# A fallback path written as a loop over short stretches, in place of unrolled blocks

## Chip, cores, metric

One core of a Trainium2 chip. The metric is the device time of one execution in microseconds (us), the median over several runs of the slowest core (here the only one). The "span" of a profile is the stretch from the first to the last recorded instruction; it is 1.5 to 2.1 us shorter than the device time of the same run.

## The reference, cut to what matters

```python
# x, f_logit: (4, 6080, 256); w_in: (256, 2048); w_out: (2048, 256)
f = lower_bound + (1 - lower_bound) * sigmoid(f_logit)
for t in range(S):                     # one recurrence along each sequence
    h = f[:, t] * h + (1 - f[:, t]) * x[:, t]
    y[:, t] = h
z = y.reshape(24320, 256) @ w_in       # 24320 tokens
out = (z - tanh(z)) @ w_out
```

Below, "h" means what the kernel calls h, the product z. For small z the kernel replaces z - tanh(z) by a short polynomial in z squared, which is exact enough; for large z it needs tanh. As built the polynomial is the cheaper way: the whole output takes 2333 us by it.

## The kernel before

It has two parts. `fast()` computes the whole output by the polynomial, and while doing so ScalarE sums max(h*h - TINY, 0) into `flags`. At the end the sum is one number, `flag`. If it is not zero, some h was too large, and `general()` computes the whole output again with tanh.

```python
TINY = 0.03
...
        def watch(n, i):
            t = half(n, i, "t")                      # h squared
            junk = sumpool.tile([P, 2, 2, HB], BF16, name="junk")
            nc.scalar.activation(
                out=junk[:, :, :, 0 : st[n]["hb"]], in_=t, func=AF.Relu, bias=-TINY,
                accum_out=flags[:, 2 * n + i : 2 * n + i + 1],
            )
...
        def end(j):                                  # the last block's output
            ...
                (nc.scalar.copy, nc.vector.tensor_copy)[half](
                    out=rows.rearrange("p i (m k) -> p i k m", k=KC), in_=bank[:]
                )
                t0 = starts[j] + half * hb
                nc.sync.dma_start(
                    out=out[t0 : t0 + hb, :].rearrange("(i p) d -> p i d", p=P), in_=rows
                )
...
    fast()
    seen = nc.values_load(flag[:].bitcast(INT32), ...)   # every engine loads the flag
    with tc.If(seen != 0):                               # every engine branches
        general()
```

`general()` runs over 48 blocks of up to 512 tokens, all unrolled in the program: 10705 instructions as built, of 23005 in all.

Of the kernel before, what the change touches and what calls it, by code (L numbers as in the profile page):

```python
# [9 lines left out]
FP32 = mybir.dt.float32  # L10
ALU = mybir.AluOpType
# [6 lines left out]
P = 128  # L18
# [13 lines left out]
def kernel(  # L32
# [25 lines left out]
    nc = tc.nc  # L58

    B, S, D = x.shape  # L60
    DFF = moe_w_in.shape[1]
    N = B * S
    KC = D // P
    TB = 512
    HB = TB // 2
    NQ = TB // P
    NU = DFF // TB
    H = 32
    G = P // H
# [4 lines left out]
    sizes = [HB] + [TB] * (N // TB)  # L74
    PLAIN, TURNED = 2, 2
    starts = [sum(sizes[:j]) for j in range(len(sizes))]
    NBLK = len(starts)
    srcs = [a.rearrange("b s d -> (b s) d") for a in (f_logit, x)]

    const = ctx.enter_context(tc.tile_pool(name="const", bufs=1))  # L80
    lb = const.tile([P, KC], FP32, name="lb")
# [832 lines left out]
    @with_exitstack  # L914
    def general(ctx):


        fetch, steps, ys = recurrence(ctx)[0:3]
        wpool = ctx.enter_context(tc.tile_pool(name="w", bufs=1))
        tpool = ctx.enter_context(tc.tile_pool(name="tpool", bufs=2))  # L920
        gpool = ctx.enter_context(tc.tile_pool(name="gpool", bufs=3))
        opool = ctx.enter_context(tc.tile_pool(name="opool", bufs=2))
        ps_h = ctx.enter_context(tc.tile_pool(name="ps_h", bufs=3, space=PSUM))
        ps_o = ctx.enter_context(tc.tile_pool(name="ps_o", bufs=1, space=PSUM))
        w_in = [wpool.tile([P, 2, 2, 2 * P], FP32, name=f"w_in{u}") for u in range(NU)]
        w_out = [wpool.tile([P, 2, 2, D], FP32, name=f"w_out{u}") for u in range(NU)]

        def temp(tag, dtype=FP32):
            return tpool.tile([P, 2, 2, HB], dtype, name=tag, tag=tag)

        with tc.manual_schedule():
            for u in range(NU):
                for fetch_w, w in ((fetch_w_in, w_in[u]), (fetch_w_out, w_out[u])):
                    raw = tpool.tile([P, KC * TB], INT64, name="raw", tag="raw")
                    fetch_w(u, raw[:], nc.gpsimd)
                    rounding = to_float32(
                        [(w[:].rearrange("p a b c -> p (a b c)"), lambda a: a)], raw[:],
                        lambda n: temp(dict(e="t", m="q", r="th")[n])[:].rearrange(
                            "p a b c -> p (a b c)"
                        ),  # L940
                    )
                    for step in ("ce", "cr", "cx", "cm", "cs", "cb", "cw"):
                        rounding[step]()
            for j, nb in enumerate(sizes):
                ns = nb // P
                fetch(j, queue=nc.gpsimd)
                for step in ("tf", "tx", "sg", "f0", "f1", "v0", "v1", "sc0", "sc1"):
                    steps[step](j)
                ps = ps_o.tile([P, NQ, D], FP32, name="psO")
                for u in range(NU):  # L950
                    for s in range(2):
                        hT = ps_h.tile([P, 2, TB], FP32, name="hT")
                        for c in range(2):
                            for k in range(KC):
                                nc.tensor.matmul(
                                    hT[:, c, 0:nb],
                                    lhsT=w_in[u][:, k, s, c * P : (c + 1) * P],
                                    rhs=ys[j][:, k, 0:nb],
                                    start=(k == 0),
                                    stop=(k == KC - 1),  # L960
                                )
                        h = hT[:, :, 0:nb]
                        t, th, q, small = [
                            temp(n)[:].rearrange("p a b c -> p a (b c)")[:, :, 0:nb]
                            for n in ("t", "th", "q", "small")
                        ]
                        gT = gpool.tile([P, 2, TB], FP32, name="gT")
                        g = gT[:, :, 0:nb]
                        nc.scalar.activation(out=t, in_=h, func=AF.Square)
                        nc.scalar.activation(out=th, in_=h, func=AF.Tanh)  # L970
                        nc.scalar.activation(
                            out=q, in_=t, func=AF.Square, scale=QA, bias=QB
                        )
                        nc.scalar.activation(
                            out=small, in_=t, func=AF.Relu, scale=-1.0, bias=SMALL
                        )
                        nc.vector.tensor_tensor(out=g, in0=h, in1=th, op=ALU.subtract)
                        nc.vector.scalar_tensor_tensor(
                            out=q, in0=q, scalar=QC, in1=th, op0=ALU.add, op1=ALU.mult
                        )  # L980
                        nc.vector.tensor_tensor(out=q, in0=q, in1=t, op=ALU.mult)
                        nc.vector.copy_predicated(
                            out=g, mask=small.bitcast(INT32), data=q
                        )
                        for c in range(2):
                            for i in range(ns):
                                nc.tensor.matmul(
                                    ps[:, i, :],
                                    lhsT=gT[:, c, i * P : (i + 1) * P],
                                    rhs=w_out[u][:, s, c, :],  # L990
                                    start=(u == s == c == 0 and i % 2 == 0),
                                    stop=(u == NU - 1 and s == c == 1),
                                    skip_group_check=True,
                                )
                osb = opool.tile([P, NQ, D], FP32, name="osb")
                nc.scalar.copy(out=osb[:, 0:ns, :], in_=ps[:, 0:ns, :])
                nc.gpsimd.dma_start(
                    out=out[starts[j] : starts[j] + nb, :].rearrange(
                        "(i p) d -> p i d", p=P
                    ),  # L1000
                    in_=osb[:, 0:ns, :],
                )

    fast()
    seen = nc.values_load(
# [3 lines left out]
    with tc.If(seen != 0):  # L1009
        general()  # L1010
# [32 lines left out]
```

## Time and profile before

| | before |
|---|---|
| device time, 3 runs | 2331.93, 2332.53, 2333.46 us |
| TensorE | busy 2319.6 us of a span of 2329.3; granted clock 1.00 |
| VectorE, ScalarE | busy 91% and 77% |
| instructions of `general()` executed | 0 |
| last output transfer | issued at 2324.4, landed 3.75 us later |

Some figures below have two decimals where a printed line has one. They are the start times of the same records in the trace, read to the nanosecond. One execution differs from the next by more than a microsecond (the spans of the changed kernel were 2329.9 to 2331.7 us), so for the last microseconds I do not compare spans. I compare distances inside one trace: from the issue of the last transfer to its landing, and to the end.

### The profile page before, as it was taken

To read this page: it belongs to the slowest core of one execution; us is meant where nothing else is said; L and a number is where in the kernel's file an instruction comes from. 1 tells how busy PE (TensorE), PEld (TensorE's weight loads), DVE (VectorE), ACT (ScalarE), POOL (GpSimd) and SP (SyncE) were. 2 spreads that over 40 slices of the span, in tenths; PEclk is the share of its full clock that TensorE was granted. 3 is DMA by queue.
4 is the path that set the end of the run, shared out by engine and by line. 5 is a ranking of instruction groups with operands and counts; after the bars stand their busy time and mean duration, and the time that the engine had idled before them with its cause. 6 is when DMAs were issued, how large, how long until landed. Compare 5 with 4: busy or idle time off the path is not lost.

```text
span 2329.3 us, 28648 instructions
## 1 busy us (share of the span) xinstructions
PE 2319.6 (100%) x10677; PEld 2025.2 (87%) x10677; DVE 2121.4 (91%) x2447; ACT 1801.1 (77%) x2686; POOL 0.7 (0%) x6
## 2 busy tenths in 40 slices
PE   9999999999999999999999999999999999999998
PEld 6888888888888888888888888888888888888887
DVE  8999899998999989999999999999899998999987
ACT  7677777777777777787777777777777777777775
POOL 0000000000000000000000000000000000000000
PEclk9999999999999999999999999999999999999999
DMA  6311211111111111112111121111211112111101
GB/s 172 64 24 32 42 37 28 28 35 39 37 28 28 37 36 37 28 28 42 32 37 28 28 45 28 37 28 28 46 29 36 28 28 46 31 33 28 28 10 29
DMA packets 296932, 85.05 MB, mean 37 GB/s; under 512 B 289872, under 2 KB 292688, under 8 KB 296784
## 3 DMA queue, kind: packets, MB, share of 16 engines
q1 hardware_dynamic: 296640, 83.14, 16.9%
q8 instruction: 85, 1.39, 0.2%
q14 instruction: 63, 0.52, 0.1%
q10 hardware_dynamic: 144, 0.00, 0.0%
HBM read 58.20 MB, written 24.90 MB: 36 GB/s over the span
## 4 chain that ended last, share of the span: by engine, by line
PE 99%; DMA 0%; SPq 0%; DVE 0%; issue 0%
PE A L383 27%; PE Qd L466 14%; PE Qa L466 14%; PE Qb L466 14%; PE D L383 14%; PE Qc L466 7%; PE B L383 7%; PE Qc L749 1%; PE Qb L749 1%; PE Qa L749 1%; PE A L682 1%; PE D L682 0%; PE Qd L682 0%; DMA xn<-in_x_dram 0%; PE B L682 0%; PE Qc L682 0%
## 5 line engine op out<-in xcount | busy, mean ns | idle before, releaser
L383 PE MATMUL A<-T,w_in 128*128 128x256 f32 x2208 | 558.8, 379 | 0.0
L383 PEld LDWEIGHTS A<-T,w_in 128*128 128x128 f32 x2208 | 419.5, 190 | 57.0
L427 DVE TENSOR_TENSOR h<-h,q 128x1024 f32<-128x1024 f32 x368 | 437.7, 1220 | 3.1
L421 DVE SCALAR_TENSOR_TENSOR q<-q,t 128x1024 f32<-128x1024 f32 x368 | 440.2, 1217 | 0.0
L414 ACT ACTIVATE q<-t 128x1024 f32<-128x1024 f32 x368 | 382.8, 1053 | 46.3 <-DVE h L427 43.4
L411 ACT ACTIVATE t<-h 128x1024 f32<-128x1024 f32 x368 | 388.7, 1057 | 3.1 <-DVE h L398 0.3
L432 ACT ACTIVATE junk<-t 128x1024 bf16<-128x1024 f32 x368 | 388.2, 1055 | 1.5
L446 DVE TENSOR_TENSOR Tg<-h 128x1024 f32<-128x1024 f32 x368 | 348.1, 946 | 6.4
L466 PE MATMUL Qb<-h,w_out 128*128 128x256 f32 x1472 | 347.7, 379 | 0.0
L466 PEld LDWEIGHTS Qb<-h,w_out 128*128 128x128 f32 x1472 | 279.7, 190 | 38.0
L466 PE MATMUL Qa<-Tg,w_out 128*128 128x256 f32 x736 | 219.0, 379 | 0.0
L466 PE MATMUL Qd<-h,w_out 128*128 128x256 f32 x736 | 219.0, 379 | 0.0
L466 PE MATMUL Qa<-h,w_out 128*128 128x256 f32 x736 | 218.9, 379 | 0.0
L466 PE MATMUL Qd<-Tg,w_out 128*128 128x256 f32 x736 | 218.9, 379 | 0.0
L395 ACT COPY h<-B 128x512 f32<-128x512 f32 x184 | 107.0, 582 | 143.2 <-PE B L383 94.4
L395 ACT COPY h<-A 128x512 f32<-128x512 f32 x184 | 107.3, 583 | 136.7 <-PE A L383 125.3
L398 DVE TENSOR_TENSOR h<-D,r 128x512 f32<-128x512 f32 x184 | 126.9, 690 | 92.9 <-PE D L383 90.8
L398 DVE TENSOR_TENSOR h<-A,r 128x512 f32<-128x512 f32 x184 | 126.3, 687 | 74.3 <-PE A L383 42.5
L395 ACT COPY r<-A 128x512 f32<-128x512 f32 x184 | 107.3, 583 | 105.9 <-PE A L383 105.9
L383 PE MATMUL D<-y,w_in 128*128 128x256 f32 x736 | 188.9, 379 | 0.0
L383 PE MATMUL B<-y,w_in 128*128 128x256 f32 x736 | 188.9, 379 | 0.0
L383 PE MATMUL A<-y,w_in 128*128 128x256 f32 x736 | 188.9, 379 | 0.0
(120 smaller groups left out, 3069.8 us busy)
## 6 DMA issues: line engine op xcount, KB each, us to landing
xn<-in_x_dram SPq DMA_DIRECT2D x184, 128.0 KB, 3.2
fn<-in_f_logit_dram SPq DMA_DIRECT2D x184, 128.0 KB, 3.1
out_dram<-osb SPq DMA_DIRECT2D x180, 128.0 KB, 2.8
raw<-in_moe_w_in_dram SPq DMA_DIRECT2D x8, 512.0 KB, 4.6
raw<-in_moe_w_out_dram SPq DMA_DIRECT2D x8, 512.0 KB, 4.8
out_dram<-osb SPq DMA_DIRECT2D x3, 256.0 KB, 3.7
fn<-in_f_logit_dram SPq DMA_DIRECT2D x1, 512.0 KB, 6.9
xn<-in_x_dram SPq DMA_DIRECT2D x1, 512.0 KB, 7.7
```

The lines of the kernel that those rows point to most:

```text
L383: nc.tensor.matmul(ps[:, c], lhsT=w_in[u][:, slot, c * P : (c + 1) * P], rhs=mixes[j][right], start=start and c == 0, stop=True, skip_grou ...
L395: nc.scalar.copy(out=dst, in_=piece(n, bank))
L398: nc.vector.tensor_tensor(out=piece(n, "h")[:, q], in0=piece(n, bank), in1=piece(n, r), op=ALU.add)
L411: nc.scalar.activation(out=half(n, i, "t"), in_=half(n, i), func=AF.Square)
L414: nc.scalar.activation(out=half(n, i, "q"), in_=half(n, i, "t"), func=AF.Square, scale=RA, bias=RB,)
L421: nc.vector.scalar_tensor_tensor(out=q, in0=q, scalar=RC, in1=t, op0=ALU.add, op1=ALU.mult)
L427: nc.vector.tensor_tensor(out=h, in0=h, in1=q, op=ALU.mult)
L432: nc.scalar.activation(out=junk[:, :, :, 0 : st[n]["hb"]], in_=t, func=AF.Relu, bias=-TINY, accum_out=flags[:, 2 * n + i : 2 * n + i + 1],)
L446: nc.vector.tensor_tensor(out=o, in0=a, in1=b, op=ALU.subtract)
L466: nc.tensor.matmul(acc[j, part][:, r, 0 : st[n]["hb"]], lhsT=w_out[u][:, slot, c * P : (c + 1) * P], rhs=piece(n, right)[:, q, c], start=( ...
L682: nc.tensor.matmul(h[c], lhsT=w_in[u][:, 2 * k + s, c * P : (c + 1) * P], rhs=ys[j][:, k, 0:nb], start=k == 0 and (c == 0 or len(banks) == 2),
L749: nc.tensor.matmul(acc[j][i // 2][:, i % 2].rearrange("p (k m) -> p k m", k=2), lhsT=plain[j, u][:, s, c, i * P : (i + 1) * P], rhs=w_out[ ...
```

## The change

The intent: the fallback path need not be 48 unrolled blocks. It becomes a hardware loop of 190 iterations, each taking 32 time steps of all four sequences (128 tokens), with the recurrence's state carried in a tile. `fast()` and the test are not touched. The core of the diff:

```diff
+    ALL = len(sizes)
+    sizes.append(B * H)                 # after NBLK = len(starts)
...
-            for j, nb in enumerate(sizes):
-                ns = nb // P
-                fetch(j, queue=nc.gpsimd)
-                for step in ("tf", "tx", "sg", "f0", "f1", "v0", "v1", "sc0", "sc1"):
-                    steps[step](j)
+            nc.vector.memset(carry[:], 0.0)
+        with tc.For_i(0, S, H) as t0:
+            with tc.manual_schedule():
+                for s, src in enumerate((f_logit, x)):
+                    nat = natpool.tile(...)
+                    part = src[:, bass.ds(t0, H), :].rearrange("j b (i c) -> i b j c", i=G)
+                    for i in range(G):
+                        nc.gpsimd.dma_start(out=nat[i * H : (i + 1) * H, 0:B, :], in_=part[i])
+                for step in ("tf", "tx", "sg", "f0", "f1", "v0", "v1"):
+                    steps[step](ALL)
+                for k in range(KC):
+                    for b in range(B):
+                        nc.vector.tensor_tensor_scan(..., initial=carry[:, k, b : b + 1], ...)
+                nc.vector.tensor_copy(out=carry[:], in_=y[:, :, :, H - 1])
...                                      # the two products as before, 128 tokens wide
+                for b in range(B):
+                    nc.gpsimd.dma_start(out=dst[b], in_=osb[b * H : (b + 1) * H])
```

As built the path shrinks from 10705 instructions to 458, the program from 23005 to 12762.

More of the change, by code (lines that the diff above doesn't have):

```diff
@@ L78 @@
     srcs = [a.rearrange("b s d -> (b s) d") for a in (f_logit, x)]
+    ALL = len(sizes)
+    sizes.append(B * H)
+    assert B * H <= P and S % H == 0
     const = ctx.enter_context(tc.tile_pool(name="const", bufs=1))
@@ L915, in general @@
     def general(ctx):
-        fetch, steps, ys = recurrence(ctx)[0:3]
+        _, steps, ys, natpool, _, nats, chan = recurrence(ctx)
         wpool = ctx.enter_context(tc.tile_pool(name="w", bufs=1))
@@ L926, in general @@
         w_out = [wpool.tile([P, 2, 2, D], FP32, name=f"w_out{u}") for u in range(NU)]
+        y = wpool.tile([P, KC, B, H], FP32, name="y")
+        carry = wpool.tile([P, KC, B], FP32, name="carry")
+        nb = B * H
         def temp(tag, dtype=FP32):
@@ L943, in general @@
                         rounding[step]()
-            for j, nb in enumerate(sizes):
-                ns = nb // P
-                fetch(j, queue=nc.gpsimd)
-                for step in ("tf", "tx", "sg", "f0", "f1", "v0", "v1", "sc0", "sc1"):
-                    steps[step](j)
-                ps = ps_o.tile([P, NQ, D], FP32, name="psO")
+        with tc.For_i(0, S, H) as t0:
+            with tc.manual_schedule():
+                for s, src in enumerate((f_logit, x)):
+                    nat = natpool.tile([P, TB // H, KC * H], FP32, name=("fn", "xn")[s])
+                    part = src[:, bass.ds(t0, H), :].rearrange("j b (i c) -> i b j c", i=G)
+                    for i in range(G):
+                        nc.gpsimd.dma_start(out=nat[i * H : (i + 1) * H, 0:B, :], in_=part[i])
+                    nats[ALL, s] = nat
+                for step in ("tf", "tx", "sg", "f0", "f1", "v0", "v1"):
+                    steps[step](ALL)
+                for k in range(KC):
+                    for b in range(B):
+                        nc.vector.tensor_tensor_scan(
+                            out=y[:, k, b], data0=chan[ALL, "f", k][:, b * H : (b + 1) * H],
+                            data1=chan[ALL, "v", k][:, b * H : (b + 1) * H],
+                            initial=carry[:, k, b : b + 1], op0=ALU.mult, op1=ALU.add,
+                        )
+                nc.vector.tensor_copy(out=carry[:], in_=y[:, :, :, H - 1])
+                ps = ps_o.tile([P, D], FP32, name="psO")[0:nb]
                 for u in range(NU):
                     for s in range(2):
-                        hT = ps_h.tile([P, 2, TB], FP32, name="hT")
+                        hT = ps_h.tile([P, 2, HB], FP32, name="hT")
                         for c in range(2):
@@ L957, in general @@
                                     lhsT=w_in[u][:, k, s, c * P : (c + 1) * P],
-                                    rhs=ys[j][:, k, 0:nb],
-                                    start=(k == 0),
+                                    rhs=y[:, k].rearrange("p j b -> p (j b)"),
+                                    start=(c == 0 and k == 0),
                                     stop=(k == KC - 1),
+                                    skip_group_check=True,
                                 )
@@ L966, in general @@
                         ]
-                        gT = gpool.tile([P, 2, TB], FP32, name="gT")
+                        gT = gpool.tile([P, 2, HB], FP32, name="gT")
                         g = gT[:, :, 0:nb]
@@ L985, in general @@
                         for c in range(2):
-                            for i in range(ns):
-                                nc.tensor.matmul(
-                                    ps[:, i, :],
-                                    lhsT=gT[:, c, i * P : (i + 1) * P],
-                                    rhs=w_out[u][:, s, c, :],
-                                    start=(u == s == c == 0 and i % 2 == 0),
-                                    stop=(u == NU - 1 and s == c == 1),
-                                    skip_group_check=True,
-                                )
-                osb = opool.tile([P, NQ, D], FP32, name="osb")
-                nc.scalar.copy(out=osb[:, 0:ns, :], in_=ps[:, 0:ns, :])
-                nc.gpsimd.dma_start(
-                    out=out[starts[j] : starts[j] + nb, :].rearrange(
-                        "(i p) d -> p i d", p=P
-                    ),
-                    in_=osb[:, 0:ns, :],
-                )
+                            nc.tensor.matmul(
+                                ps,
+                                lhsT=gT[:, c, 0:nb],
+                                rhs=w_out[u][:, s, c, :],
+                                start=(u == s == c == 0),
+                                stop=(u == NU - 1 and s == c == 1),
+                            )
+                osb = opool.tile([P, D], FP32, name="osb")
+                nc.scalar.copy(out=osb[0:nb], in_=ps)
+                dst = out.rearrange("(j t) d -> j t d", j=B)[:, bass.ds(t0, H), :]
+                for b in range(B):
+                    nc.gpsimd.dma_start(out=dst[b], in_=osb[b * H : (b + 1) * H])
     fast()
```

## The prediction

> **What bounds the kernel now.** I read the page's busy shares first, then the chain that ended last, then the busy time of each engine by stretches, and last the sequencer instructions of the final microseconds, because the change sits behind a branch that is taken there.
>
> ```profile
> span 2329.3 us, 28648 instructions
> PE 2319.6 (100%) x10677; PEld 2025.2 (87%) x10677; DVE 2121.4 (91%) x2447; ACT 1801.1 (77%) x2686; POOL 0.7 (0%) x6
> PEclk9999999999999999999999999999999999999999
> ...
> PE 99%; DMA 0%; SPq 0%; DVE 0%; issue 0%
> ```
>
> TensorE is busy from end to end, at full granted clock, and is 99% of the chain that ended last. In the stretches:
>
> ```profile
> core 0: us, PE busy (x) PEld busy (x) DVE busy (x) ACT busy (x) POOL busy (x), PEclk, DMA share, GB/s
> 600.00:1200.00 600.00, 600.00 (x2782) 528.18 (x2781) 550.59 (x624) 468.93 (x696) 0.00 (x0) 1.00 0.16 33
> 1200.00:1800.00 600.00, 600.00 (x2782) 528.18 (x2781) 548.74 (x622) 468.52 (x696) 0.00 (x0) 1.00 0.17 34
> 2280.00:2330.00 50.00, 43.27 (x204) 37.32 (x202) 37.14 (x44) 27.51 (x42) 0.00 (x0) 0.97 0.10 27
> ```
>
> 600 us over 2782 matmuls is 216 ns each, with no gap. Nothing but fewer or shorter matmuls could speed up the middle. Only the last line has slack: TensorE stops about 6 us before the span's end.
>
> The question is then whether anything that the change edits is executed. It edits only the path for large h, entered when a flag summed at the end is not zero. Asked for that path's accumulator tile (psO), the trace answers:
>
> ```profile
> nothing on psO; most used: ['w_out', 'w_in', 'h', 'A', 'T', 'y', 'Tg', 'D', 'Qa', 'Qb', 'Qd', 't', 'B', 'Qc', 'q', 'r', 'junk', 'C', 'fT', 'fn', 'xn', 'osb', 'f', 'v', 'in_f_logit_dram']
> ```
>
> POOL's six instructions on the page are start-up constants, so none of the path's work ran. With these inputs the flag is zero and the whole path is jumped over. What runs of it is the branch itself, line 1009, and the landing behind it, line 1039:
>
> ```profile
> L1009 POOLq COMPARE_BRANCH  x1: 45/45/45, 2321.3 to 2321.3; - x1
> L1009 PEldq COMPARE_BRANCH  x1: 3711/3711/3711, 2323.7 to 2323.7; - x1
> L1009 ACTq COMPARE_BRANCH  x1: 50/50/50, 2323.7 to 2323.7; - x1
> L1009 DVEq COMPARE_BRANCH  x1: 72/72/72, 2324.3 to 2324.3; - x1
> L1009 SPq COMPARE_BRANCH  x1: 50/50/50, 2325.6 to 2325.6; - x1
> L1009 ACTq EVENT_SEMAPHORE  x1: 17/17/17, 2326.5 to 2326.5; - x1
> L1009 PEldq EVENT_SEMAPHORE  x1: 51/51/51, 2327.4 to 2327.4; - x1
> L1009 DVEq EVENT_SEMAPHORE  x1: 21/21/21, 2327.6 to 2327.6; - x1
> ```
>
> The columns are instruction, count, shortest/median/longest ns, first and last start. TensorE's branch takes 3711 ns; ScalarE's starts at 2323.7 and its next instruction at 2326.5; VectorE's at 2324.3 and 2327.6: a hole of about 2.7 to 3.7 us on each engine that jumps far. SyncE, which has one instruction to jump over, goes on 0.2 us later.
>
> Do these holes set the end? The waits of the last queue say no:
>
> ```profile
> L541 SPq DMA_DIRECT2D out_dram<-osb x2: 389/389/389, 2323.8 to 2324.4; - x2
> DMA to landing us min/median/max: 3.7/3.7/3.8
> ...
> SPq L1039 <- DMA out_dram<-osb: 1.9, 2, 1.4
> SPq L1039 <- PEq L1039: 0.7, 2, 0.5
> ```
>
> The last output transfer is issued at 2324.4 and lands 3.8 us later, at 2328.2; SyncE waits for that, 1.9 us in two waits. TensorE and VectorE have passed their branches by 2327.4 and 2327.6, so the holes have about 0.5 us of slack. From 2328.2 to 2329.3 runs the closing barrier.
>
> [...] The page's DMA part has
>
> ```profile
> q8 instruction: 85, 1.39, 0.2%
> q14 instruction: 63, 0.52, 0.1%
> ```
>
> which is 16.4 KB a packet on one queue and 8.3 KB on the other[...].
>
> **The change part by part.**
> 1. The fast part, all that runs before the branch. I compared both built programs: this block has 12228 instructions in each, in the same order, with the same operands, semaphores and buffer addresses; no instruction differs except in its running name. The new entry in the list of block sizes is appended after the number of blocks is taken, so no tile changes. Cost 0.
> 2. The path for large h. It shrinks from 10705 instructions as built (4629 of them TensorE's) to some 450 with its loop. None runs before, and none will, since the flag comes from an identical part: 0 instructions times any duration, 0 us. That it would do 190 short iterations instead of 48 blocks matters to other inputs alone.
> 3. Set-up. The new program has four more register moves on GpSimd ahead of the start barrier, for addresses computed at run time. Such sequencer steps take about 20 to 50 ns in the trace; all engines wait for that barrier, so plus 0.1 to 0.2 us, exposed.
> 4. The branch. TensorE jumped over 4629 built instructions; a float32 matmul is issued as two loads and two matmuls (10677 recorded for 5363 built), so some 18000[...]. Now it is about 223[...]. ScalarE goes from 2375 to about 100, VectorE from 2991 to about 150, GpSimd from 709 to about 95. I expect most of the holes to close. That takes 3.7 us off TensorE's own tail, but the end waits for the output transfer at 2328.2, so directly 0 us.
> 5. What may still come through. [...] In the record of packets most engines' parts of these transfers are through by 2326.2 to 2326.6, while one that carried a 16 KB fetch (1.24 us, from 2324.7) goes on to 2327.8. Without that fetch I would expect landing up to 1.2 us sooner (an estimate: 2327.8 less 2326.6). [...] I count half: minus 0.6 us.
> Sum: 0 + 0 + 0.15 - 0.6, about -0.5 us. On the median of 2332.5 that is 2332.0.
>
> **The rivals.**
> - The holes are exposed after all. If the end followed TensorE's branch, closing it would bring up to 3.7 us, to about 2329. Against: SyncE's waits name the DMA, and that lands 0.5 us after the last hole. Even so it is 0.16%, within 2%.
> - The compiler laid the fast part out anew (other addresses, other bank or order), moving the 216 ns or opening waits. [...] the comparison of the builds shows nothing to start from.
> - The loop costs something at the end: SyncE had 1 instruction to jump over and now has about 37, so it may [...] get a hole of some 2.7 us as ScalarE did. It comes after its last issue of a transfer and beside the flight of that transfer, so it would end at about 2325.6 + 2.7 = 2328.3, some 0.1 us past the landing: under 1 us, to 2333 at most.
> - The path is entered after the change. It would add hundreds of us or more; against it, the identical instructions that make the flag.
>
> **Range and chances.** The three runs before lie from 2331.93 to 2333.46, 1.5 us. The steps above span -3.7 to +1 us, mostly -1.2 to +0.5. Spread and steps together give 2329.5 to 2334.2. A change of 2% is 47 us, more than ten times the whole tail; only a re-laid fast part or an entered path reaches it. I give 0.98 to within 2% and 0.01 to each side.
>
> **What would show it right or wrong.** Right: again 28648 or so instructions, 10677 matmuls and 216 ns in the middle stretches; nothing on psO; TensorE's branch well under 1 us, and ScalarE, VectorE and GpSimd going on within some 0.2 us of theirs; SyncE still waiting for the output transfer last; the instruction queues within a few packets of 85 and 63. Step 5 is right if that transfer lands in clearly less than 3.7 us and the span shrinks by as much. Wrong: a branch as long as before (then nearness isn't what counts), another matmul cadence, or a span that moves by more than 4 us on the same chip.

## The result, and the profile after

| | before | after |
|---|---|---|
| device time, median of 6 runs each | 2332.30 us | 2332.78 us |
| lowest to highest | 2331.25 to 2333.46 | 2331.47 to 2333.26 |

The ratio is 1.0001 with a 95% interval of 0.9988 to 1.0014: the same. The outputs are right. (A ratio is the mean time of one kernel's fast runs over that of the other's of the same rounds, so not quite the ratio of the medians.)

The page of the changed kernel, the lines that answer to those of before:

```profile
span 2329.9 us, 28652 instructions
PE 2319.6 (100%) x10677; PEld 2025.3 (87%) x10677; DVE 2121.4 (91%) x2447; ACT 1801.0 (77%) x2686; POOL 0.7 (0%) x6
...
PE 99%; DMA 0%; SPq 0%; DVE 0%; issue 0%
```

Every engine has the same count of working instructions and, within 0.1 us, the same busy time. The span has four instructions more. Asked for the path's tile psO, the trace again has nothing on it.

The branch is now line 1026 and the landing behind it line 1056. Columns: engine and instruction, count, shortest/median/longest ns, first and last start:

```profile
L1026 PEldq COMPARE_BRANCH  x1: 361/361/361, 2324.0 to 2324.0; - x1
L1026 ACTq COMPARE_BRANCH  x1: 45/45/45, 2324.1 to 2324.1; - x1
L1026 ACTq EVENT_SEMAPHORE  x1: 17/17/17, 2324.2 to 2324.2; - x1
L1026 PEldq EVENT_SEMAPHORE  x1: 51/51/51, 2324.4 to 2324.4; - x1
L1026 DVEq COMPARE_BRANCH  x1: 72/72/72, 2324.7 to 2324.7; - x1
L1026 DVEq EVENT_SEMAPHORE  x1: 21/21/21, 2325.3 to 2325.3; - x1
```

TensorE's branch fell from 3711 to 361 ns. From a branch to the engine's next instruction it is now 0.42 us on TensorE (before 3.77), 0.18 on ScalarE (2.72), 0.59 on VectorE (3.25) and 0.47 on GpSimd (2.69). So the far jump cost each of these four engines 2.2 to 3.4 us more than the near one does, and that is gone. Yet the end did not come sooner:

```profile
L545 SPq DMA_DIRECT2D out_dram<-osb x2: 389/389/389, 2324.2 to 2324.8; - x2
DMA to landing us min/median/max: 4.0/4.0/4.1
...
SPq L1056 <- DMA out_dram<-osb: 2.2, 2, 1.6
SPq L1056 <- PEq L1056: 0.7, 2, 0.5
```

The waits of SyncE's queue again name the output transfer, now for 2.2 us in place of 1.9, because it takes 4.06 us to land in place of 3.75. The start moved too. The first transfer that SyncE issues, in the timeline of before and then of after (start, duration, instruction), with the instructions that came in ahead of it:

```profile
0.75 0.67 SPq L103 DMA_DIRECT2D raw<-in_moe_w_in_dram  x1
```

```profile
L1041 POOLq MOVE  x4: 29/29/35, 0.2 to 0.4; - x4
...
0.98 0.67 SPq L107 DMA_DIRECT2D raw<-in_moe_w_in_dram  x1
```

Four register moves on GpSimd stand ahead of the start barrier. SyncE, ScalarE, VectorE and TensorE pass that barrier at 0.67 to 0.68 us before and at 0.90 to 0.92 after, so everything starts 0.24 us later. The profiled spans differ by 0.62 us: 0.24 of it is this start; from the last issue to the end it is 5.19 us against 4.89, another 0.30; the 0.08 left arose between the two, and I did not trace it.

So two questions stay after the result. The holes of some 3 us are gone: were they really hidden, as the prediction says? And the fetches were to delay the landing: why does it take longer now, 4.06 us in place of 3.75?

### The profile page after: what moved, and what is told of

The parts are those of the page before. It is cut to its first block, busy times and chain, and to the rows that moved or that the text cites. A ratio compares the mean times of both kernels' runs of the same rounds, so it can differ in the third digit from the quotient of the medians.

```text
span 2329.9 us, 28652 instructions
## 1 busy us (share of the span) xinstructions
PE 2319.6 (100%) x10677; PEld 2025.3 (87%) x10677; DVE 2121.4 (91%) x2447; ACT 1801.0 (77%) x2686; POOL 0.7 (0%) x6
## 4 chain that ended last, share of the span: by engine, by line
PE 99%; DMA 0%; SPq 0%; DVE 0%; issue 0%
PE A L387 27%; PE Qd L470 14%; PE Qa L470 14%; PE D L387 14%; PE Qb L470 14%; PE Qc L470 7%; PE B L387 7%; PE Qa L753 1%; PE Qc L753 1%; PE Qb L753 1%; PE A L686 1%; PE D L686 0%; PE Qd L686 0%; DMA xn<-in_x_dram 0%; PE B L686 0%; PE Qc L686 0%
```

## The experiments

My theory: the time before the branch cannot change, because nothing there differs; the holes are hidden behind the landing of the last output; that landing is slow because TensorE's instruction fetch runs beside it. By that fetch I mean a packet of queue q8, which the DMA view lists as instruction; each has 16384 B in the traces of before and after, and near_shift shows below that they go with TensorE. Rivals: the holes are simply free; the flag loads, or two transfers in flight at once, make the landing slow; the landing varies by chance. Most runs are single looks, to be read by distances within their traces; nopath had three rounds and the two forced kernels one. A single look has no state of its own; its granted clock was 0.998 or more in each (the forced kernels apart).

The main distances of all kernels whose last transfer is whole and ends the run, worked out from start times in the traces, in us:

| kernel | first SyncE issue | TensorE branch to its next instruction | branch to the start of TensorE's fetch | last issue to landing | last issue to end |
|---|---|---|---|---|---|
| before | 0.75 | 3.77 | 1.06 | 3.75 | 4.89 |
| after | 0.98 | 0.42 | 1.76 | 4.06 | 5.19 |
| near | 0.74 | 0.42 | 1.09 | 3.58 | 4.69 |
| nopath | 0.74 | no branch | no fetch | 2.35 | 3.37 |
| load_only | 0.74 | no branch | no fetch | 2.36 | 3.41 |
| near_shift | 0.74 | 0.42 | 1.08 | 3.90 | 5.01 |
| after_shift | 0.99 | 0.42 | 1.08 | 3.78 | 4.91 |
| loop_sync | 0.76 | 0.42 | 1.10 | 4.05 | 5.92 |
| near_late | 0.74 | 0.42 | 1.09, over before the issue | 2.15 | 3.26 |

### near: a short path without a loop

The kernel before, with its path cut to a stub of one unit of one block, unrolled. It would give a wrong result if it ran; it does not run.

```diff
-            for u in range(NU):                 # the path's weights
+            for u in range(1):
-            for j, nb in enumerate(sizes):
+            for j, nb in enumerate(sizes[:1]):
-                for u in range(NU):
+                for u in range(1):
```

> The kernel before, with its path for large h cut down to a stub (one unit of one block; wrong if it ran, but it does not run). Theory: nearness of the target closes the holes and the four register moves come from the loop's run-time addresses. So the start barrier stays where it was before (first SyncE issue at 0.75 us, not 0.98), TensorE's branch takes under 0.5 us (before 3.71), VectorE goes on within 0.7 us (before 3.2), and the end does not come earlier: second output issue to end 4.7 to 5.4 us (before 4.89, after 5.19). Rival, the fetches delay the last transfer: second issue to end at most 4.0 us. Rival, the loop itself (not its length) closed the holes: TensorE's branch again near 3.7 us.

The first issue stays at 0.74 us and TensorE's branch takes 367 ns, so the holes go with the length of the jump and not with the loop. The end is 4.69 us behind the last issue, sooner than before by only 0.2 us, and at the lower edge of what I wrote. The rival that closing the holes brings the end to 4.0 us falls.

### nopath: no flag test, no branch, no path

```diff
-    seen = nc.values_load(flag[:].bitcast(INT32), ...)
-    with tc.If(seen != 0):
-        general()
```

> The changed kernel without flag test, branch and path. Theory (what bounds is TensorE and then the landing of the output): time the same, within 2 us of the kernel before; start as before (0.75 us); second issue to end 4.6 to 5.3 us. Rival (the branch or the path's code costs something on the way): 3 us or more faster, the end within 3.5 us of the second issue.

2330.55 us against 2331.35, ratio 0.9995, interval 0.9978 to 1.0011: the same time. But the end came 3.37 us behind the last issue, which my theory had at 4.6 to 5.3: a miss (the rival's "within 3.5 us" fits, though not its gain of 3 us), and the most useful one, since the transfer landed after 2.35 us in place of 3.6 to 4.1. The DMA view from the last issue to the end, of near and then of nopath (queue, packets, MB, share of the engines):

```profile
q1 hardware_dynamic: 544, 0.52, 32.3%
q8 instruction: 1, 0.02, 1.7%
```

```profile
q1 hardware_dynamic: 544, 0.52, 44.3%
```

The same 544 packets of output. In near one 16 KB packet of instructions on queue q8 runs beside them; in nopath none does. nopath also has two transfers in flight at once, so that alone does not make the landing slow.

### before_short and after_short: what the holes are worth when nothing hides them

In both kernels the last two transfers are cut to two rows each, so that they land soon (in SyncE's waits, listed down to 0.4 and 0.3 us, no landing of them is left; in before it was 1.9 us). Their outputs are wrong, which doesn't matter for the times.

```diff
-                    out=out[t0 : t0 + hb, :].rearrange("(i p) d -> p i d", p=P), in_=rows
+                    out=out[t0 : t0 + hb, :].rearrange("(i p) d -> p i d", p=P)[0:1],
+                    in_=rows[0:1],
```

> The kernel before with the last two output transfers cut to two rows each (wrong result on purpose), so that they land in about 2 us in place of 3.7. Theory: now the far branch sets the end. VectorE goes on 3.2 us after its branch, the end comes 1.0 to 1.2 us behind that: second issue to end 4.1 to 4.4 us. Rival (holes cost nothing at all): second issue to end 3.0 to 3.3 us, what the shorter landing alone would give.

> The changed kernel with the same cut of the last transfers (wrong result on purpose). Theory: holes are closed, so the end follows the short landing: second issue to end 2.9 to 3.3 us, about 1 us less than the kernel before with the same cut. Rival (the change is worth nothing even where the landing is short): the same as that kernel, 4.1 to 4.4 us.

From the last issue to the end: 3.87 us with the far branch, 3.36 with the near one. Both lie outside what I wrote, since issuing these small transfers took SyncE 0.62 to 0.76 us each in place of 0.39. That put off both the last issue, from which I count, and SyncE's own way to the end. The sign is as expected, and SyncE's waits say why. In the kernel before, cut short, it waits for VectorE behind its branch:

```profile
SPq L1040 <- PEq L1040: 0.7, 2, 0.5
SPq L1040 <- DVEq L1010: 0.4, 1, 0.4
```

The changed kernel, cut short, has no such wait. So the far jump is worth 0.4 to 0.5 us, and only where the landing is short; with the real transfer it is hidden.

### load_only: the flag is loaded, nothing branches

```diff
-    with tc.If(seen != 0):
-        general()
+    assert seen is not None
```

> The changed kernel without branch and path, but with the five loads of the flag into registers. In the kernel without flag and path the last transfer landed 2.4 us after its issue, with no instruction fetch in the tail; in all others with a whole last transfer it took 3.6 to 4.1. Theory (a page of TensorE's instructions, fetched beside the transfer, delays it): no fetch here either, so landing 2.2 to 2.6 us. Rival (the loads of the flag delay it): 3.5 us or more with no fetch in the tail.

Landing 2.36 us, no fetch in the tail. The loads of the flag are not what delays it.

### near_shift and after_shift: another place in the stream of instructions

Queue q8 has its 16 KB packets all through the run: in near three of them (from 2213.68 to 2296.36 us) go with 767 TensorE records, about 256 each. I took TensorE's fetch in the tail for one more of this stream (an assumption, which these runs refute), and moved the stream by adding instructions: at the start, where TensorE waits for data and runs warming matmuls, 37 (25 in after_shift) short ones in place of 7 long.

```diff
-            for _ in range(n):
+            w = 7 * TB // 37 if n == 7 else TB
+            for _ in range(37 if n == 7 else n):
                 nc.tensor.matmul(
-                    busy[:], lhsT=zeros.bitcast(BF16)[:, 0:P],
-                    rhs=zeros.bitcast(BF16)[:, 0:TB], start=True, stop=True,
+                    busy[:, 0:w], lhsT=zeros.bitcast(BF16)[:, 0:P],
+                    rhs=zeros.bitcast(BF16)[:, 0:w], start=True, stop=True,
```

> The stub kernel with 60 more TensorE instructions at the start (37 short warming matmuls in place of 7 long ones, as many columns), so that [...] TensorE's last page is fetched some 5 us earlier, before the last transfers. Theory (the page fetch delays the landing): no 16 KB fetch after the issue of the last transfer, landing 2.2 to 2.7 us after it, end 3.3 to 3.8 us after it (stub alone: 3.6 and 4.7), TensorE's branch without a hole. Rival (flag loads, or just chance): landing again 3.5 us or more.

> The changed kernel with 36 more TensorE instructions at the start (25 short warming matmuls in place of 7), the same reason. Theory: TensorE's fetch leaves the tail and the landing falls from 4.1 to at most 3.2 us; an 8 KB fetch of another engine at the end may hold some of it back. Rival (only chance, or the 8 KB fetches): 3.5 us or more.

Both missed: landing 3.90 and 3.78 us. The instructions, added on TensorE alone, did move the fetches of the stream on q8, so it is TensorE's: the last but one began at 2290.91 us in near_shift, at 2296.36 in near. But the last one did not leave the tail. It began 1.08 us after TensorE's branch in both, as in near. TensorE's record holds 328 instructions from the fetch before it to this one in near_shift, and 272 in near. So it did not come at a fixed count of instructions; it followed the branch. The idea that a shift could avoid it fell.

### loop_sync: the loop's transfers on SyncE's queue

```diff
-                        nc.gpsimd.dma_start(out=nat[i * H : (i + 1) * H, 0:B, :], in_=part[i])
+                        nc.sync.dma_start(out=nat[i * H : (i + 1) * H, 0:B, :], in_=part[i])
-                    nc.gpsimd.dma_start(out=dst[b], in_=osb[b * H : (b + 1) * H])
+                    nc.sync.dma_start(out=dst[b], in_=osb[b * H : (b + 1) * H])
```

> The changed kernel with the loop's transfers on SyncE's queue in place of GpSimd's. The built program has no more the four register moves ahead of the start barrier. Theory (they are what moves the start): first SyncE issue back at 0.73 to 0.75 us (changed kernel 0.98). Rival (a loop in the program moves the start in any case): 0.9 us or more. The end as in the changed kernel, give or take 0.5 us; SyncE jumps further and may get a hole of up to 2.7 us, hidden beside the flight of the output.

The four moves are gone from GpSimd, and the first issue is at 0.76 us. They are not gone from the program: they now stand on SyncE, whose transfers have the run-time addresses instead.

```profile
L1041 SPq MOVE  x4: 29/34/42, 0.0 to 0.2; - x4
```

There they are over by 0.22 us, while the barrier opens at 0.67 us, after GpSimd's last step ahead of it (0.63), so they delay next to nothing. So it was the moves on GpSimd, not the loop, that cost the 0.24 us. The end is 0.7 us later than in the changed kernel, outside what I wrote. SyncE did not get a hole; it now has eight more semaphore waits on the way around the path (from 2327.32 to 2330.22 us, the last five of them waiting for the two landings or coming after them), so this is no gain either.

### near_late: the transfer after the fetch

The stub kernel again, with the two last evictions done six times each. The result is the same; the transfers are issued 2.0 and 2.4 us later in the trace than in near, and 3.4 to 4.4 us after TensorE's branch in place of 0.2 to 0.8.

```diff
-                (nc.scalar.copy, nc.vector.tensor_copy)[half](
-                    out=rows.rearrange("p i (m k) -> p i k m", k=KC), in_=bank[:]
-                )
+                for _ in range(6):
+                    (nc.scalar.copy, nc.vector.tensor_copy)[half](
+                        out=rows.rearrange("p i (m k) -> p i k m", k=KC), in_=bank[:]
+                    )
```

> The stub kernel with the two last evictions repeated six times each (same result), so that the last transfers are issued 3 us later, when the page that TensorE fetches after its branch is in. Theory (that fetch, beside the transfer, is what delays it): flag loads and branches are all there, the fetch starts about 1.1 us after TensorE's branch and ends before the transfer's first packets, and the landing falls to 2.2 to 2.6 us (stub: 3.6; without branch: 2.4). Rival (the branches or something else in the tail delay it): 3.4 us or more.

The issue and landing of the last transfers, and the DMA view from the first issue to the end:

```profile
L542 SPq DMA_DIRECT2D out_dram<-osb x2: 388/388/389, 2327.3 to 2328.3; - x2
DMA to landing us min/median/max: 2.1/2.2/2.2
...
q1 hardware_dynamic: 544, 0.52, 35.5%
```

All flag loads and all branches are there, those of ScalarE, VectorE and SyncE still beside the transfers. Only TensorE's branch with its fetch (2324.95 to 2326.26 us) is over, as is GpSimd's, which in near too came 2.6 us ahead of the issue; no q8 line is left in the window. The landing falls from 3.58 to 2.15 us, just below the range that I wrote. The two transfers lie 0.98 us apart here and 0.58 in near, so some of this may come from the spacing; nopath, with 0.58, landed in 2.35, which puts that part at about 0.2 us (an estimate: 2.35 less 2.15).

### before_forced and after_forced: the path taken

The limit lowered, so that the flag is set. Both results were right.

```diff
-TINY = 0.03
+TINY = 0.0001
```

> The kernel before with the limit on h squared lowered from 0.03 to 0.0001, so that the flag is set and the path for large h runs (results must still be right). From the shares of the trace I estimate 14 us for each of 8 units of a block of 512 (TensorE 6.9 us, and some 7 us of ScalarE and VectorE that nothing covers) and 12 us of head: 124 us times 47.5, 5.9 ms on top of 2.3: about 8.2 ms. It is to show that the path is where the change is, and that the flag is what kept it from the time.

> The changed kernel with the same lowered limit. Estimate: some 4 us for each of 8 units of 128 tokens, and 25 us of loads, transposes, output and loop barrier that nothing covers: 57 us times 190, 10.8 ms on top of 2.3: about 13 ms, so 1.3 to 2 times the kernel before with the same limit. Theory: the change is a trade of code size against the time of a path that these inputs never take. Rival (the loop is as good as the blocks): within 10% of it.

9685.35 and 14424.59 us (ratios to the kernel before 4.15 and 6.18). Less the 2332.61 us of the fast part of the same runs, the path takes 7353 us unrolled and 12092 us as a loop, 1.64 times as long. My estimates, 5.9 and 10.8 ms, were too low: 124 us a block against 155 measured (7353 over 47.5), and 57 us an iteration against 64 (12092 over 190). One likely reason is that they took TensorE at the full clock of the fast part (1.00). The kernel before's row of granted clock (PEclk, one digit per slice, in tenths) shows 6 to 7 for most of the path:

```profile
PEclk9999999998666666666666666666766666666666
```

Where the loop loses, by groups of both (line, engine, operation, tiles, shapes, count, then busy us and mean ns, then idle before):

```profile
L955 PE MATMUL hT<-y,w_in 128*128 128x512 f32 (+1 forms) x3072 | 1472.9, 625 | 785.7 <-DVE y L227 785.7
L977 DVE TENSOR_TENSOR gT<-hT,th 128x1024 f32<-128x1024 f32 (+1 forms) x384 | 466.0, 1213 | 4297.0 <-ACT th L970 4297.0
```

```profile
L976 PE MATMUL hT<-y,w_in 128*128 128x128 f32 x12160 | 2802.3, 407 | 3050.6 <-DVE y L964 3050.6
L999 DVE TENSOR_TENSOR gT<-hT,th 128x256 f32<-128x256 f32 x1520 | 644.8, 424 | 5927.5 <-ACT th L992 5927.5
```

Four times as many instructions of a quarter of the width, each costing a third to two thirds of the wide one; and the first layer's idle time before it, waiting for the recurrence at the head of each iteration, grows from 786 to 3051 us. The granted clock differs too: it was 0.69 in the unrolled path (2400 to 9600 us) and 0.61 in the loop (2400 to 14400 us), so not all of the 1.64 need be the form of the loop; no run separates the two. On these inputs none of it is ever executed.

The two traces also bear on what sets off TensorE's fetch. Here TensorE reaches the same branch and does not take it: the branch took 78 ns, and no packet on q8 began in the next 50 us (the next one came 53 us later in before_forced, and only at the program's end in after_forced). So here the fetch goes with the jump around the path, not with the branch as such. Nor did every jump bring one: in after_forced TensorE went back to the head of the loop 189 times without a fetch.

## Why the prediction was right, point by point

The predicted time was 2332.0 us; measured 2332.78, within the range, with the kernel before at 2332.30.

1. The fast part costs nothing: right. The counts of working instructions are equal and the busy times agree within 0.1 us.
2. The path costs nothing: right. Nothing of it ran; forced to run, it would cost 4.7 ms more than before.
3. The set-up: right in kind, mis-sized. The term was 0.1 to 0.2 us; it measured 0.24. The prediction went by the time that such a step takes (29 to 35 ns here), but from the start of one move to the next it was 0.06 us. loop_sync shows that the moves are the cause where they stand on GpSimd.
4. The branch: right. Most of the holes closed on all four engines, SyncE got none (0.19 us from its branch to its next instruction), and the end did not follow. TensorE's branch took 361 to 367 ns in after, near, after_short and loop_sync, 3711 and 3747 ns in before and before_short. Its own time shows the hole on TensorE alone: ScalarE's far branch took 50 ns and its near one 45, while its next instruction came 2.72 and 0.18 us after the start of the branch. One sign was missed: VectorE and GpSimd were to go on within some 0.2 us and took 0.59 and 0.47; with the still shorter path of near they took 0.23 and 0.17. The slack that the prediction gives the holes, about 0.5 us, is 0.6 in the trace (from VectorE's 2327.58 to the landing at 2328.18). That the holes were hidden is shown by before_short and after_short, where they cost 0.4 to 0.5 us once the landing is short.
5. What may come through, minus 0.6 us: this step failed. "Without that fetch I would expect landing up to 1.2 us sooner": near_late, and the two kernels without a branch, land (2.15 to 2.36 us) 1.2 to 1.9 us sooner than those with TensorE's fetch beside the transfer (3.58 to 4.06), so the late landing and the fetch do go together. But the step counted half of it as gained, by estimate, and none of it was. In every run of the table in which TensorE jumped around the path, a 16 KB packet began on q8 1.06 to 1.76 us after the branch, also where TensorE went on after 0.42 us. With the near branch the fetch was therefore still beside the transfer, and the landing took 4.06 us in place of 3.75. The kernels with a near branch lie from 3.58 to 4.06 us, and the 3.75 of before lies among them, so the 0.31 itself is no more than their scatter.

The sum was -0.5 us; the medians moved +0.5 us, inside the noise of runs that spread over 2 us. That is a right verdict with one wrong term too small to matter.

What stays open: how, and whether, the fetch itself delays the landing. In near it ended at 2327.45 us. Of the 544 packets of output 515 had ended by 2327.83; the last 29 ended one after another, most of them 0.04 us apart, up to 2329.02. In nopath all had ended by 2328.00. In the kernel before a chain of 31, each starting as the one before it ends, runs from 2326.31 to 2327.77 us; the 16 KB packet had ended at 2325.96. One of 16 engines would have 34 of the packets (544 over 16), so this looks like one engine's share waiting behind the fetch, as the prediction had it; the trace does not name the engine, so that one engine carried both is an estimate and not shown. Against the 2.35 us of nopath the landing is 1.2 us late in near, where the 16 KB packet took 1.3 us, but 1.7 us late in the changed kernel, where it took 0.9, so the packet's own time does not explain the whole delay. In the changed kernel an 8 KB packet of the other instruction queue, q14 (0.52 us), ran beside the transfer too; what that adds was not tested. Nor can TensorE's jump and its fetch be told apart as causes of the late landing: the forced kernels have no fetch there, but the path's own loads run beside their transfers (landing 4.3 to 8.1 us). It is not shown either why the fetch in the changed kernel's first profile began 1.76 us after the branch and not 1.1 (after_shift: 1.08).

No kernel here beats both. Dropping the guard gains nothing that the times can tell from noise, and would be wrong for other inputs; loop_sync saves 0.23 us at the start and loses more at the end.

## What to carry to other kernels

Before costing a change, ask the trace whether the changed lines are executed at all, and ask the build whether the executed part differs; here both answers were no, and the rest was a matter of half a microsecond. What code that is not run can still do is change the length of the jump around it, which if far cost 2.2 to 3.4 us more per engine here, and bring set-up instructions ahead of the start (0.24 us here with four moves on GpSimd, no more than 0.02 with the same four on SyncE). Whether such a hole matters is decided by what ends last beside it (here it cost nothing beside a landing of 3.75 us, and 0.4 to 0.5 us beside a short one); and the size of a fallback path is then to be weighed against its own time when it is taken, here 1.64 times as long.
